# All four gate groups of the last chunk ahead of its value groups

## The chip, the cores and the metric

The kernel runs on one core of one Trainium2 chip. The metric is device time in microseconds (us) of one execution; less is better. Beside it stands a profile of one execution, whose span runs from the first to the last recorded instruction. Engines are called PE (TensorE, matmuls), PEld (its weight loads), DVE (VectorE), ACT (ScalarE), POOL (GpSimd) and SP (SyncE, which here issues transfers). L551 is line 551 of the kernel.

## The reference

An attention over 32 memory slots, followed by a channel mix with a gate. The change lies in the channel mix:

```python
def _moe_ref(x, mu_k, mu_r, w_k, w_v, w_r):
    x_prev = np.concatenate([np.zeros((B, 1, D)), x[:, :-1, :]], axis=1)
    xk = mu_k * x + (1.0 - mu_k) * x_prev
    xr = mu_r * x + (1.0 - mu_r) * x_prev
    k = np.maximum(xk @ w_k, 0.0)
    v = k * k @ w_v
    r = 1.0 / (1.0 + np.exp(-(xr @ w_r)))
    return (r * v).astype(np.float32)
```

Here x is the attention's output with 8 batches of 576 tokens and 512 channels, w_k is 512 x 1024, w_v 1024 x 512 and w_r 512 x 512. Tokens are independent once xk and xr are there.

## The kernel before

Attention runs per batch and writes xk and xr, transposed and in bf16, into two rings in on-chip memory. The channel mix works through the 4608 tokens in NCH = 9 chunks of 512. Each chunk has 16 groups of work, one per step of a schedule:

- eight **key** groups k0 to k7 (L510 to L524): 128 of the 1024 inner channels each. PE makes `pk` (L518, 4 matmuls of 512 columns), ACT takes the ReLU (L522), DVE squares it into `sq` (L523).
- four **gate** groups g0 to g3 (L526 to L541): 128 tokens each. PE makes `pr` (L532, 4 matmuls), ACT reads it with an exponential (L537). After every second gate ACT finishes the pair's sigmoids `sg` with a logarithm (L539) and an exponential (L540) over both.
- four **value** groups v0 to v3 (L543 to L555): 128 tokens each. PE makes `pv` from `sq` (L551, 8 matmuls), DVE multiplies it with the gate into `o` (L553), and `store` sends `o` to memory. In the last chunk v3 is made in two halves of 256 columns, each with its own accumulator, product and stores.

The schedule is a list of steps with positions, sorted before anything is emitted (L562 to L572). Channel mix step s stands at position s, so chunk c has positions 16c to 16c + 15. Attention steps have positions written out by hand in FIRST and STEADY, relative to their batch: those of the last batch reach position 118 at most, and the last chunk, c = 8, begins at 128. Within each engine instructions run in the order in which they are emitted. The order of gates and values within a chunk is the string on L558.

Accumulators come from tags with a fixed number of buffers, taken in turn: `pk` has two, `at` (attention) three, and gates and values share the three of tag `pv` (L529, L549). A group that takes a buffer waits until its previous user has been read: a gate's by L537, a value's by L553. `sg` has two buffers of two gates each, `sq` one for a chunk, and `o` three (L545); a value group waits until the stores of the value group three before it have landed.

`store` (L490 to L502) splits a block of 128 tokens into pieces by where they lie in the output; here each block has two. SP issues them all, except that for the last two blocks of the program (v2 and v3 of the last chunk) the second piece goes to ACT's queue:

```python
            eng.dma_start(out=dst, in_=o[p:p + n, cols])
            if t >= NTOK // 128 - 2:
                eng = nc.scalar
```

So the last chunk has ten stores: two each of v0, v1 and v2, and two for each half of v3.

Of the kernel before, what the change touches and what calls it, by code (L numbers as in the profile page):

```python
# [62 lines left out]
def kernel(  # L63
# [27 lines left out]
    NCH = NTOK // CT  # L91
# [398 lines left out]
    def store(o, t, cols):  # L490
        g = t * 128
        eng = nc.sync
        while g < (t + 1) * 128:
            b, r = divmod(g, S)
            p = g - t * 128
            j, p0 = divmod(r, QR)
            n = min(QR - p0, (t + 1) * 128 - g)
            dst = out[b].rearrange("(p j) d -> p j d", j=NQ)[p0:p0 + n, JT[j], cols]
# [3 lines that stand above are left out]
            g += n  # L502

    def channel_mix(c):
        t0 = c * CT
        wrap = RING - t0 % RING
        pieces = [(0, CT)] if wrap >= CT else [(0, wrap), (wrap, CT)]
        st = {}

        def key(fi):  # L510
            def go():
                if "sq" not in st:
                    st["sq"] = work.tile([128, NF, CT], BF16, name="sq", tag="sq", bufs=1)
                pk = psum.tile([128, CT], F32, name="pk", tag="pk", bufs=2)
                for lo, hi in pieces:
                    c0 = (t0 + lo) % RING
                    for di in range(ND):
                        nc.tensor.matmul(pk[:, lo:hi], lhsT=wk_sb[:, di, fi * 128:(fi + 1) * 128],  # L518
                                         rhs=xk_T[:, di, c0:c0 + hi - lo],
                                         start=(di == 0), stop=(di == ND - 1))  # L520
                rl = work.tile([128, CT], BF16, name="rl", tag="rl", bufs=3)
                nc.scalar.activation(rl, pk, AF.Relu)  # L522
                nc.vector.tensor_mul(st["sq"][:, fi, :], rl, rl)  # L523
            return go  # L524

        def gate(ts):  # L526

            def go():
                pr = psum.tile([128, Dm], F32, name="pr", tag="pv", bufs=3)  # L529
                c0 = (t0 + ts * 128) % RING  # L530
                for di in range(ND):
                    nc.tensor.matmul(pr, lhsT=xr_T[:, di, c0:c0 + 128],  # L532
                                     rhs=wr_sb[:, di, :], start=(di == 0), stop=(di == ND - 1))
                if ts % 2 == 0:
                    st[ts // 2] = work.tile([128, 2, Dm], F32, name="sg", tag="sg", bufs=2)
                sg = st[ts // 2]
                nc.scalar.activation(sg[:, ts % 2], pr, AF.Exp, scale=-1.0)  # L537
                if ts % 2 == 1:
                    nc.scalar.activation(sg, sg, AF.Ln, bias=1.0)  # L539
                    nc.scalar.activation(sg, sg, AF.Exp, scale=-1.0)  # L540
            return go  # L541

        def value(ts):  # L543
            def go():
                o = work.tile([128, Dm], F32, name="o", tag="o", bufs=3)  # L545
                n = 2 if c == NCH - 1 and ts == 3 else 1
                for h in range(n):
                    cols = slice(h * Dm // n, (h + 1) * Dm // n)
                    pv = psum.tile([128, Dm], F32, name="pv", tag="pv", bufs=3)  # L549
                    for fi in range(NF):  # L550
                        nc.tensor.matmul(pv[:, cols], lhsT=st["sq"][:, fi, ts * 128:(ts + 1) * 128],  # L551
                                         rhs=wv_sb[:, fi, cols], start=(fi == 0), stop=(fi == NF - 1))
                    nc.vector.tensor_mul(o[:, cols], st[ts // 2][:, ts % 2, cols], pv[:, cols])  # L553
                    store(o, t0 // 128 + ts, cols)
            return go  # L555

        groups = [key(fi) for fi in range(NF)]
        order = "g0 g1 g2 g3 v0 v1 v2 v3" if c == 0 else "g0 g1 v0 v1 g2 g3 v2 v3"  # L558
        return groups + [(gate if o[0] == "g" else value)(int(o[1])) for o in order.split()]


# [5 lines left out]
    for s in range(16 * NCH):  # L567
        if s % 16 == 0:
            groups = channel_mix(s // 16)
        todo.append((s, -1, 0, groups[s % 16]))  # L570
# [32 lines left out]
```

The softmax here doesn't subtract the row's maximum and nothing guards it: scores larger than these inputs give would overflow.

## Time and profile before

| | us |
|---|---|
| median of 4 runs | 224.73 (224.24 to 225.82) |
| the profiled execution | 224.94 |
| its span | 223.1 |
| PE busy in the span | 205.9 (92%) |
| ACT busy | 160.0 (72%) |
| DVE busy | 142.4 (64%) |
| 320 key matmuls, L518 | 69.4 |
| 144 gate matmuls, L532 | 35.2 |
| 296 value matmuls, L551 | 66.3 |

The granted clock of PE is full throughout (1.000). A matmul's recorded length (358 to 379 ns) is longer than its spacing, since matmuls overlap. In the chain of waits, which counts each stretch once, 8 gate matmuls in a row take 1.73 us and 16 value matmuls 3.45 us.

The lines shown below are of four kinds. A timeline row has its start, the time that the merged instructions took, engine, line, operation, output and input, and in brackets how long the engine had been idle and what released it. A row of stages has start and end, then for each engine busy time and number of instructions, the granted clock, the DMA engines' busy share and GB/s. A row of one line's instructions gives the least, median and greatest duration in ns and the first and last start. An engine with a q at its end (SPq, ACTq) is that engine's queue of issued transfers.

### The profile page before, as it was taken

What the parts mean: (1) busy time and instruction counts of PE and PEld (TensorE: products, weight loads), DVE (VectorE), ACT (ScalarE), POOL (GpSimd) and SP (SyncE); (2) the same over time, 40 slices, a digit from 0 to 9 for tenths busy, and PEclk for the clock granted to TensorE, in tenths of its full rate; (3) what the DMA queues carried; (4) which work ended last, traced back from release to release, by engine and by line L of the source; (5) the groups of instructions that cost most, each with busy time, mean ns of one, the idle gap of its engine ahead of it and who ended that gap; (6) DMA issues with size and microseconds to landing.
All of it is one profiled execution on the core that took longest, in us unless ns stands there. A gap on an engine that the chain in (4) does not pass through costs nothing.

```text
span 223.1 us, 4576 instructions
## 1 busy us (share of the span) xinstructions
PE 205.9 (92%) x1755; PEld 101.7 (46%) x1755; DVE 142.4 (64%) x356; ACT 160.0 (72%) x309; POOL 47.6 (21%) x66
## 2 busy tenths in 40 slices
PE   4269999899999998999999999999999999999991
PEld 1243345445444554445445764444443444444450
DVE  3162855297456989688777698769875974435222
ACT  2107568982899849997799679977978856855760
POOL 7554351644240638122500000000000000000000
PEclk9999999999999999999999999999999999999999
DMA  6999999999999999999994300330132033033033
GB/s 133 189 200 207 235 204 212 224 223 276 218 238 198 265 209 204 232 205 299 132 187 103 94 3 0 94 97 1 33 102 58 0 94 94 3 94 94 0 94 94
DMA packets 43349, 31.49 MB, mean 141 GB/s; under 512 B 10952, under 2 KB 37840, under 8 KB 43328
## 3 DMA queue, kind: packets, MB, share of 16 engines
q0 software_dynamic: 35248, 20.91, 62.7%
q1 hardware_dynamic: 7776, 9.97, 15.7%
q10 hardware_dynamic: 304, 0.33, 0.4%
q8 instruction: 13, 0.21, 0.4%
q14 instruction: 8, 0.07, 0.1%
HBM read 38.54 MB, written 9.44 MB: 215 GB/s over the span
## 4 chain that ended last, share of the span: by engine, by line
PE 80%; ACT 6%; DVE 5%; DMA 3%; POOL 1%; issue 1%; SPq 1%; DVEq 0%; POOLq 0%
PE pk L518 28%; PE pv L551 25%; PE pr L532 13%; DMA mu_b<-in_moe_mu_r_dram 3%; PE qtps L325 2%; PE kvps L264 2%; PE nops L382 2%; PE idle L209 2%; PE zps L355 2%; PE scps L341 1%; DVE atn L369 1%; PE mxps L439 1%; DVE o L553 1%; ACT e L345 1%; PE zps L274 1%
## 5 line engine op out<-in xcount | busy, mean ns | idle before, releaser
L518 PE MATMUL pk<-xkT,wk 128*128 128x512 bf16 (+1 forms) x320 | 69.4, 358 | 0.0
L551 PE MATMUL pv<-wv,sq 128*128 128x512 bf16 (+1 forms) x296 | 66.3, 373 | 0.0
L522 ACT ACTIVATE rl<-pk 128x512 bf16<-128x512 f32 x72 | 43.1, 601 | 27.0 <-PE pk L518 26.7
L523 DVE TENSOR_TENSOR sq<-rl 128x512 bf16<-128x512 bf16 x72 | 30.4, 423 | 25.9 <-ACT rl L522 25.5
L553 DVE TENSOR_TENSOR o<-sg,pv 128x512 f32<-128x512 f32 (+1 forms) x37 | 24.0, 672 | 31.6 <-ACT sg L540 25.6
L551 PEld LDWEIGHTS <-sq 128*128 128x128 bf16 x296 | 28.6, 98 | 32.0 <-issue 0.2
L518 PEld LDWEIGHTS <-wk 128*128 128x128 bf16 x320 | 29.0, 98 | 26.2 <-issue 1.6
L532 PE MATMUL pr<-wr,xrT 128*128 128x512 bf16 x144 | 35.2, 379 | 0.0
L537 ACT ACTIVATE sg<-pr 128x512 f32<-128x512 f32 x36 | 21.8, 605 | 8.6 <-PE pr L532 8.4
L532 PEld LDWEIGHTS <-xrT 128*128 128x128 bf16 x144 | 13.3, 98 | 15.9 <-issue 1.2
L539 ACT ACTIVATE sg<-sg 128x1024 f32<-128x1024 f32 x18 | 19.0, 1057 | 0.6
L540 ACT ACTIVATE sg<-sg 128x1024 f32<-128x1024 f32 x18 | 19.0, 1057 | 0.6
L345 ACT ACTIVATE e<-scps 128x288 bf16<-128x288 f32 x32 | 10.8, 428 | 8.1 <-PE scps L341 8.1
L407 DVE TENSOR_SCALAR mu_d<-diff,mu 128x576 bf16<-128x576 bf16 x48 | 16.4, 383 | 0.2
L386 ACT CAST x<-nops 128x288 bf16<-128x288 f32 x48 | 16.0, 416 | 0.0
L328 DVE COPY qT<-qtps 128x576 bf16<-128x576 bf16 x32 | 13.4, 450 | 1.3 <-PE qtps L325 1.3
L369 DVE TENSOR_TENSOR atn<-e,lz 128x576 bf16<-128x576 bf16 (+1 forms) x20 | 12.3, 634 | 2.9 <-ACT lz L362 2.5
L325 PE MATMUL qtps<-identity,q 96*128 96x96 bf16 x192 | 12.4, 215 | 1.2 <-DMA q<-in_q_dram 1.2
L325 PEld LDWEIGHTS <-q 96*128 96x128 bf16 x192 | 10.9, 103 | 4.7 <-DMA q<-in_q_dram 1.4
L357 ACT ACTIVATE lz<-zps 128x288 f32<-128x288 f32 x32 | 11.2, 412 | 1.2 <-PE zps L355 1.2
L362 ACT ACTIVATE lz<-lz 128x576 f32<-128x576 f32 (+1 forms) x20 | 11.4, 596 | 0.0
L248 ACT ACTIVATE em<-phm 128x1024 bf16<-128x1024 f32 x8 | 8.4, 1055 | 3.2 <-DMA phm<-in_phi_dram 3.2
(66 smaller groups left out, 187.2 us busy)
## 6 DMA issues: line engine op xcount, KB each, us to landing
out_dram<-o SPq DMA_DIRECT2D x23, 192.0 KB, 2.3
kv<-in_k_dram POOLq DMA_DIRECT2D x8, 512.0 KB, 12.4
q<-in_q_dram POOLq DMA_DIRECT2D x7, 576.0 KB, 15.0
phm<-in_phi_dram POOLq DMA_DIRECT2D x7, 512.0 KB, 12.9
kv<-in_v_dram POOLq DMA_DIRECT2D x7, 512.0 KB, 13.2
out_dram<-o SPq DMA_DIRECT2D x23, 128.0 KB, 2.4
out_dram<-o SPq DMA_DIRECT2D x23, 64.0 KB, 2.0
wk<-in_moe_w_k_dram POOLq DMA_DIRECT2D x2, 512.0 KB, 12.6
```

The source lines that it names most:

```text
L325: nc.tensor.matmul(ps[:, i, j], rhs=identity[:QR, :QR], is_transpose=True, lhsT=qs[b % 2][:, 2 * pr + i, 2 * j:2 * j + 2, :].rearrange("p ...
L386: nc.scalar.copy(st["x"][:, 2 * c + jj, sl], pss[jj])
L407: nc.vector.tensor_scalar_mul(t[:, i], st["d"][:, pr + i, :], mu1[:, o:o + 1])
L518: nc.tensor.matmul(pk[:, lo:hi], lhsT=wk_sb[:, di, fi * 128:(fi + 1) * 128], rhs=xk_T[:, di, c0:c0 + hi - lo], start=(di == 0), stop=(di = ...
L522: nc.scalar.activation(rl, pk, AF.Relu)
L523: nc.vector.tensor_mul(st["sq"][:, fi, :], rl, rl)
L532: nc.tensor.matmul(pr, lhsT=xr_T[:, di, c0:c0 + 128], rhs=wr_sb[:, di, :], start=(di == 0), stop=(di == ND - 1))
L537: nc.scalar.activation(sg[:, ts % 2], pr, AF.Exp, scale=-1.0)
L539: nc.scalar.activation(sg, sg, AF.Ln, bias=1.0)
L540: nc.scalar.activation(sg, sg, AF.Exp, scale=-1.0)
L551: nc.tensor.matmul(pv[:, cols], lhsT=st["sq"][:, fi, ts * 128:(ts + 1) * 128], rhs=wv_sb[:, fi, cols], start=(fi == 0), stop=(fi == NF - 1))
L553: nc.vector.tensor_mul(o[:, cols], st[ts // 2][:, ts % 2, cols], pv[:, cols])
```

## The change

In the last chunk, the order of the eight groups behind the keys becomes that of the first chunk: all four gates, then all four values. No other chunk and no instruction of a group is edited.

```diff
         groups = [key(fi) for fi in range(NF)]
-        order = "g0 g1 g2 g3 v0 v1 v2 v3" if c == 0 else "g0 g1 v0 v1 g2 g3 v2 v3"
+        order = "g0 g1 g2 g3 v0 v1 v2 v3" if c in (0, NCH - 1) else "g0 g1 v0 v1 g2 g3 v2 v3"
         return groups + [(gate if o[0] == "g" else value)(int(o[1])) for o in order.split()]
```

## The prediction

> **What bounds the kernel now.** I read the page first: busy shares, then the chain that ended last, to see which engine a moved group could free.
>
> ```profile
> PE 205.9 (92%) x1755; PEld 101.7 (46%) x1755; DVE 142.4 (64%) x356; ACT 160.0 (72%) x309; POOL 47.6 (21%) x66
> PE 80%; ACT 6%; DVE 5%; DMA 3%; POOL 1%; issue 1%; SPq 1%; DVEq 0%; POOLq 0%
> ```
>
> PE is the bound of the whole, and the change gives it the same matmuls. So only two things can move: gaps on PE inside the last chunk, and what follows PE's last matmul. The next view is busy time by stage: keys of the last chunk (200.90 on), its first half, its second half, the stores, the close of the program.
>
> ```profile
> 200.90:207.80 6.90, 6.90 (x33) 3.14 (x32) 3.46 (x9) 4.18 (x7) 0.00 (x0) 1.00 0.29 76
> 207.80:213.00 5.20, 5.20 (x25) 2.35 (x24) 1.29 (x3) 3.90 (x5) 0.00 (x0) 1.00 0.00 0
> 213.00:218.20 5.20, 5.17 (x32) 2.94 (x30) 1.36 (x4) 3.31 (x4) 0.00 (x0) 1.00 0.33 101
> 218.20:221.80 3.60, 0.00 (x0) 0.00 (x0) 0.70 (x3) 0.00 (x0) 0.00 (x0) 1.00 0.50 146
> 221.80:223.10 1.30, 0.00 (x0) 0.00 (x0) 0.00 (x0) 0.00 (x0) 0.00 (x0) 1.00 0.00 0
> ```
>
> After the span's start and the length come PE, PEld, DVE, ACT and POOL, then the granted clock, the DMA share and GB/s. PE has no gap from 200.9 to 218.2, so the change can take none away. But 4.9 us lie behind PE's last matmul. The timeline of the last chunk shows what they wait for.
>
> ```profile
> 209.56 0.60 ACT L537 ACTIVATE sg<-pr 128x512 f32<-128x512 f32 x1 [0.27 <-PE pr L532]
> 210.19 1.06 ACT L539 ACTIVATE sg<-sg 128x1024 f32<-128x1024 f32 x1
> 211.28 1.06 ACT L540 ACTIVATE sg<-sg 128x1024 f32<-128x1024 f32 x1
> 212.36 1.34 DVE L553 TENSOR_TENSOR o<-sg,pv 128x512 f32<-128x512 f32 x2 [3.48 <-ACT sg L540]
> 212.81 1.89 PE L532 MATMUL pr<-wr,xrT 128*128 128x512 bf16 x8
> ...
> 214.74 0.60 ACT L537 ACTIVATE sg<-pr 128x512 f32<-128x512 f32 x1 [0.27 <-PE pr L532]
> 215.37 1.06 ACT L539 ACTIVATE sg<-sg 128x1024 f32<-128x1024 f32 x1
> 216.46 1.06 ACT L540 ACTIVATE sg<-sg 128x1024 f32<-128x1024 f32 x1
> 217.54 1.35 DVE L553 TENSOR_TENSOR o<-sg,pv 128x512 f32<-128x512 f32 x3 [3.84 <-ACT sg L540]
> ```
>
> The second half's gates leave PE at 214.7; ACT takes until 217.52 to make the sigmoids. The sums of v2 were complete near 216.43 and wait for ACT, not PE. So three products start together at 217.54, and three pairs of stores follow close behind. The instructions of the storing line from 219.3 on, with the least, median and greatest duration in ns:
>
> ```profile
> L499 SPq DMA_DIRECT2D out_dram<-o x2: 372/450/528, 218.8 to 219.5; - x2
> L499 ACTq DMA_DIRECT2D out_dram<-o x2: 392/566/739, 218.9 to 219.8; - x2
> DMA to landing us min/median/max: 2.0/2.2/2.4
> ```
>
> The last product ends at 218.90, yet its ACT store starts only at 219.75: it stands behind the stores of v2 (218.26, 0.56 us) and of v3's first half (218.91, 0.74 us). It lands at 219.75 + 2.0, near 221.8, and the closing 1.3 us follow.
>
> **What the Trainium skill says.** "PSUM — Partial Sum Buffer", Specifications: eight banks, 512 FP32 values each. The code's tags (3 `at`, 2 `pk`, 3 `pv`) take all eight; the fourth gate therefore reuses a bank. The same page, Engine vs sequencer instructions: the queues of ScalarE and VectorE are strict FIFO. The trace agrees: ACT runs L537, L537, L539, L540 in program order. "Perfetto Trace Analysis", DMA Instruction — HWDGE: the profiled length of an issue is descriptor generation, not data movement. The trace agrees: v2's issue ends at 218.73, while the DMA share is zero until 219. "DMA: Bandwidth & Descriptors", Issuing engines are not separate DMA queues: stores from SP and ACT share the same 16 DMA engines. Here their share was 0.92 to 0.98 from 219.5 to 221.0.
>
> **The change part by part.** No instruction is added or removed. In chunk 8, g2 and g3 (8 matmuls, 1.73 us in the chain) move ahead of v0 and v1 (16 matmuls, 3.45 us). ACT's eight gate instructions keep their order; DVE's five products and the ten stores (seven issued by SP, the last three others by ACT) keep theirs too. All attention steps of the last batch have positions below 128, where this chunk's first key group stands, so nothing else is crossed; POOL's queue is empty here.
>
> PE, from the pitch of 0.216 us a matmul: g0 and g1 end at 209.52 as before; g2 at 210.39, g3 at 211.25, v0 at 212.98. The ring of three banks goes g0 A, g1 B, g2 C, g3 A, v0 B, v1 C, v2 A, v3's halves B and C. g3 wants A at 210.22; ACT read it by 209.29. v0 wants B at 211.09, free at 210.16. v1 wants C, g2's bank, at 212.81. That is the one new wait: g2's L537 is ready to run at 210.4 but stands behind the first pair's L539 and L540, so it runs 212.37 to 212.97 (0.60). A wake-up was 0.03 (ACT end 217.52 to DVE 217.54), so v1 starts near 213.0: **PE loses 0.2 us**. The trace does not show this wait. Below I bound it by 0.15 (the read alone), above by 0.4 (a weight load of 0.1 and a slow wake-up of 0.1 on top). Queued behind it on PE are v1 to v3, whose delay I carry through. All later banks are free: A after g3's L537 at 213.60 for v2 at 214.7; B after v0's product at 213.7 for v3 at 216.5; C after v1's product at 215.6 for 217.3.
>
> ACT: 212.97 + 0.03 + 0.60 + 0.03 + 1.06 + 0.03 + 1.06 puts the second pair's sigmoids at 215.8, 1.7 us earlier than 217.52. So v2 to v3 now wait for PE.
>
> DVE and stores, with 0.2 of delay: v2's sums end at 216.63, product (0.69) to 217.35, stores from 217.38, SP busy to 217.85, ACT to 217.94. v3's first half: PE 217.50, product (0.41) to 217.95, stores from 217.98; SP is free at 218.51, ACT (0.74) at 218.72, and 0.1 lies between two issues on it. v3's second half: PE 218.37, product to 218.82, both stores at 218.85. **The last store starts 0.90 earlier** (219.75 - 218.85): 0.08 of it from the product, the rest because its queue is free by then. The first of the six, v2's, starts 0.88 earlier (218.26 - 217.38), so even if the DMA engines and not the issues set the end, the same 512 KB begin and end about 0.9 earlier.
>
> Output buffers: v3's `o` reuses v0's, which waits for v0's stores; these start at 213.7 and 214.2 and land within 2.3, by 216.5, and v3 wants it at 217.5: 1.0 us of cover; if that were gone, the excess would fall on the end one for one. v0's product itself moves from 212.36 to 213.0; nobody waits for it but that buffer and bank B.
>
> Landing: I keep 2.0 us, the value of the same store before, since the six stores follow each other as closely as before. Bounds: 1.6, the least of this line's stores (then 1.3 us gained in all), and 2.5, near the 2.7 of the worst (then 0.4 gained). Then the closing 1.3 us, unchanged.
>
> Sum: span 223.1 - 0.9 = 222.2. The profiled execution took 224.94, so 1.84 lie around the span, and the same execution would take 224.04; the median of the runs, 224.73, is 0.21 below that execution, so **223.8**. PE's stall is already inside the 0.9.
>
> **The rivals.** A: the forecast, 223.8, 60%. B: the last stores land in 1.6; gain 1.3, **223.4**, 21%. For it: SP's last store now has 0.3 us free ahead of it and ACT's 0.1, so the engines may have drained more of the earlier ones. Against it: the six still start within 1.5 us, as before. C: the saved issue time is hidden anyway: the last store lands as late after the product as it did before (221.8 - 218.90 = 2.9), because the engines and not the queue made it late; then only the product's 0.08 is left, **224.6**, 12%. For it: DMA share above 0.9 after 219.5; against it: the transfers begin 0.88 earlier as well. D, slower: v1's bank is not freed by g2's first ACT pass but by the end of ACT's second pair, at 215.8 (if the bank order or the wait reaches to g3's whole sequence). PE would then stall 215.8 - 212.8 = 3.0 instead of 0.2, and the end comes 2.8 - 0.9 = 1.9 later: **226.6**, 7%. It costs more than it brings from a stall of 1.1 on. Against it: before, v1 reused g0's bank although L539 and L540 of that pair had not finished, with no gap on PE. That the order isn't changed at all can be excluded: the diff replaces the string for exactly this chunk.
>
> **How the numbers follow.** The range is 223.2 to 224.6: gains of 0.4 to 1.3 us give 223.4 to 224.3, widened by 0.2 to 0.3 for the scatter of a median (runs from 224.24 to 225.82), and it takes in B and C. A change of 0.5%, 1.12 us, is about what a measurement of this kernel can tell from none; faster than that means below 223.61. Of A's 60 about 19 lie there (a landing of 1.8 or less, or the scatter), of B's 21 about 20: faster 39%. Slower is D less a remainder of mild cases: 6%. The rest, 55%, is within.
>
> **What would show it.** On PE one gap of about 0.2 us ahead of v1 near 212.8, released by ACT L537, and none else in the chunk. L540's last pass ending near 215.8. DVE's product of v2 near 216.7, released by PE, and the last product ending near 218.8. First stores on ACT at 217.4, the last at 218.9, landing near 220.9; a span of 222.2. The forecast is wrong if the last store still starts after 219.3, if its landing takes 2.7 or more, or if PE stalls for over 1 us.

## The result, and the profile after

The changed kernel took 224.05 us in the median of 31 runs (223.16 to 225.2); beside them the kernel before took 225.33 in 50 runs (224.2 to 226.35). The ratio is 0.9951, with a 95% interval of 0.9940 to 0.9961: about 1.1 us less. (The two medians, over unequal numbers of runs, differ by 1.28 us; the text goes by the ratio.) The span of the profiled execution fell from 223.1 to 222.0 us.

First the busy shares of the changed kernel, then its stages: keys, the first and second part of the gates and values, the landing of the last stores, the close of the program. The columns are those of the same view before.

```profile
PE 206.0 (93%) x1755; PEld 101.8 (46%) x1755; DVE 142.6 (64%) x356; ACT 159.7 (72%) x309; POOL 47.7 (21%) x66
```

```profile
200.90:207.80 6.90, 6.90 (x33) 3.13 (x32) 3.44 (x8) 4.39 (x8) 0.00 (x0) 1.00 0.29 76
207.80:213.00 5.20, 5.20 (x25) 2.33 (x24) 0.60 (x2) 4.60 (x7) 0.00 (x0) 1.00 0.00 0
213.00:218.20 5.20, 4.98 (x31) 2.84 (x29) 2.48 (x5) 2.17 (x3) 0.00 (x0) 1.00 0.35 102
...
218.50:220.70 2.20, 0.00 (x0) 0.00 (x0) 0.00 (x0) 0.00 (x0) 0.00 (x0) 1.00 0.68 208
220.70:222.00 1.30, 0.00 (x0) 0.00 (x0) 0.00 (x0) 0.00 (x0) 0.00 (x0) 1.00 0.00 0
```

PE has the same work. What moved is ACT and DVE: ACT's busy time in the stage up to 213 grew from 3.90 to 4.60 us and in the next fell from 3.31 to 2.17, while DVE's in that stage grew from 1.36 to 2.48. The products were spread over the last microseconds instead of standing at their end. The timeline of the changed kernel's last chunk shows it:

```profile
209.94 1.06 ACT L539 ACTIVATE sg<-sg 128x1024 f32<-128x1024 f32 x1
210.62 1.82 PEld L551 LDWEIGHTS <-sq 128*128 128x128 bf16 x9
210.84 7.14 PE L551 MATMUL pv<-wv,sq 128*128 128x512 bf16 x40
211.03 1.06 ACT L540 ACTIVATE sg<-sg 128x1024 f32<-128x1024 f32 x1
211.99 1.07 ACT L537 ACTIVATE sg<-pr 128x512 f32<-128x512 f32 x2
...
213.09 1.06 ACT L539 ACTIVATE sg<-sg 128x1024 f32<-128x1024 f32 x1
213.54 5.25 SPq L499 DMA_DIRECT2D out_dram<-o  x7
214.18 1.06 ACT L540 ACTIVATE sg<-sg 128x1024 f32<-128x1024 f32 x1
...
216.33 1.24 DVE L553 TENSOR_TENSOR o<-sg,pv 128x512 f32<-128x512 f32 x2 [1.10 <-PE pv L551]
217.05 1.87 ACTq L499 DMA_DIRECT2D out_dram<-o  x3
218.02 0.42 DVE L553 TENSOR_TENSOR o<-sg,pv 128x256 f32<-128x256 f32 x1 [0.45 <-PE pv L551]
```

The second pair's sigmoids end at 214.18 + 1.06 = 215.24. The product of v2 starts at 216.33 and is released by PE, where before it started at 217.54 and was released by ACT. The first store on ACT leaves at 217.05 instead of 218.26. The last, from the instructions of the storing line between 218.2 and 219.0, leaves at 218.5 instead of 219.75:

```profile
L499 ACTq DMA_DIRECT2D out_dram<-o x2: 390/557/724, 217.7 to 218.5; - x2
L499 SPq DMA_DIRECT2D out_dram<-o x1: 317/317/317, 218.5 to 218.5; - x1
DMA to landing us min/median/max: 2.0/2.2/2.4
```

One thing has to be taken out before two executions are compared. The chain of waits of the changed kernel says where the gates begin, that is, where the keys of the last chunk end:

```profile
204.96 2.59 PE pk L518 x12
207.55 3.45 PE pr L532 x16
211.00 6.99 PE pv L551 x40
```

Before, that point was 207.79:

```profile
207.79 1.73 PE pr L532 x8
```

So 0.24 of the 1.1 us between the spans had come about ahead of the change. I call the time from that point to the end of the span the tail; from the trace's records it is 15.34 us before and 14.50 after, 0.84 less. Times of single stores, here and below, are read from the same records.

### The profile page after: what moved, and what is told of

The parts are those of the page before. It is cut to its first block, busy times and chain, and to the rows that moved or that the text cites. A ratio compares the mean times of both kernels' runs of the same rounds, so it can differ in the third digit from the quotient of the medians.

```text
span 222.0 us, 4576 instructions
## 1 busy us (share of the span) xinstructions
PE 206.0 (93%) x1755; PEld 101.8 (46%) x1755; DVE 142.6 (64%) x356; ACT 159.7 (72%) x309; POOL 47.7 (21%) x66
## 4 chain that ended last, share of the span: by engine, by line
PE 82%; DVE 5%; ACT 4%; DMA 3%; POOL 1%; issue 1%; SPq 1%; DVEq 0%; POOLq 0%
PE pk L518 28%; PE pv L551 27%; PE pr L532 13%; DMA mu_b<-in_moe_mu_r_dram 3%; PE qtps L325 2%; PE kvps L264 2%; PE nops L382 2%; PE idle L209 2%; PE zps L355 2%; PE scps L341 1%; PE mxps L439 1%; DVE atn L369 1%; DVE o L553 1%; ACT e L345 1%; PE zps L274 1%
## 5 line engine op out<-in xcount | busy, mean ns | idle before, releaser
L553 DVE TENSOR_TENSOR o<-sg,pv 128x512 f32<-128x512 f32 (+1 forms) x37 | 24.2, 672 | 31.3 <-ACT sg L540 18.3
L537 ACT ACTIVATE sg<-pr 128x512 f32<-128x512 f32 x36 | 21.6, 604 | 6.8 <-PE pr L532 6.5
L540 ACT ACTIVATE sg<-sg 128x1024 f32<-128x1024 f32 x18 | 19.0, 1057 | 0.6
L539 ACT ACTIVATE sg<-sg 128x1024 f32<-128x1024 f32 x18 | 19.0, 1057 | 0.6
L369 DVE TENSOR_TENSOR atn<-e,lz 128x576 bf16<-128x576 bf16 (+1 forms) x20 | 12.3, 633 | 2.9 <-ACT lz L362 2.5
## 6 DMA issues: line engine op xcount, KB each, us to landing
kv<-in_k_dram POOLq DMA_DIRECT2D x8, 512.0 KB, 12.3
wk<-in_moe_w_k_dram POOLq DMA_DIRECT2D x2, 512.0 KB, 12.3
```

## The experiments

The theory: the second pair's sigmoids used to be late, and all six last stores with them. The rivals put the gain on PE's order, on a wait that any chunk has, on the DMA engines rather than the queues, or ahead of the last chunk. Each ratio is to the kernel before, run on the same chip. "Keys end" is the first gate matmul in the chain of waits. A tail comes from one trace each. How far it repeats can be seen twice: "again" is within 0.07 us of the changed kernel, and chunk7, whose last chunk is that of the kernel before, is within 0.06 of the kernel before.

| run | ratio, 95% interval | keys end, us | tail, us |
|---|---|---|---|
| kernel before | 1 | 207.79 | 15.34 |
| changed kernel | 0.9951 (0.9940 to 0.9961) | 207.55 | 14.50 |
| again | 0.9961 (0.9948 to 0.9974) | 207.71 | 14.43 |
| pass1 | 0.9966 (0.9949 to 0.9983) | 207.79 | 14.48 |
| pass2 | 1.0003 (0.9985 to 1.0020) | 208.59 | 15.59 |
| chunk7 | 1.0008 (0.9988 to 1.0028) | 207.41 | 15.40 |
| mid | 0.9968 (0.9951 to 0.9985) | 207.90 | 14.51 |
| sp_only | 1.0001 (0.9981 to 1.0021) | 208.48 | 15.37 |
| halves | 0.9957 (0.9937 to 0.9976) | 207.88 | 14.20 |
| halves_b | 0.9999 (0.9978 to 1.0021) | 207.28 | 15.50 |
| exps | 0.9959 (0.9943 to 0.9974) | 208.13 | 14.30 |
| both | 0.9941 (0.9915 to 0.9968) | 208.38 | 14.17 |

**A dose of the lateness: pass1 and pass2.** Into the changed kernel, with n = 1 or 2:

```diff
                 nc.scalar.activation(sg[:, ts % 2], pr, AF.Exp, scale=-1.0)
+                if c == NCH - 1 and ts == 3:
+                    for _ in range(n):
+                        spare = work.tile([128, 2, Dm], F32, name="spare", tag="spare", bufs=1)
+                        nc.scalar.activation(spare, sg, AF.Exp)
```

> The changed kernel with one more ACT pass (about 1.0 us, into a spare tile) between g3's exponential and the second pair's L539. Theory (the gain is that the second pair's sigmoids are ready before v2's sums): they end near 216.3 instead of 215.2, still level with v2's sums at 216.3, so nothing is lost: ratio to the kernel before 0.995 to 0.996. Rival (any ACT work behind the gates is on the path to the end): the whole pass is paid, ratio 0.999 to 1.000.

> The same with two more passes. Theory: the sigmoids end near 217.2, so v2's product waits 0.9 us for ACT as in the kernel before, the stores start 0.9 later and nearly the whole gain is gone: ratio 0.999 to 1.000. Rival (the gain comes from the order of the matmuls on PE and its buffers, not from ACT): it stays at 0.995 to 0.996.

Timelines of the two kernels near v2's product, where L544 is the old L540 and L557 the old L553; pass1 first:

```profile
213.33 1.06 ACT L541 ACTIVATE spare<-sg 128x1024 f32<-128x1024 f32 x1
...
215.51 1.06 ACT L544 ACTIVATE sg<-sg 128x1024 f32<-128x1024 f32 x1
216.60 1.21 DVE L557 TENSOR_TENSOR o<-sg,pv 128x512 f32<-128x512 f32 x2 [1.12 <-ACT sg L544]
```

```profile
214.13 2.15 ACT L541 ACTIVATE spare<-sg 128x1024 f32<-128x1024 f32 x2
...
217.40 1.06 ACT L544 ACTIVATE sg<-sg 128x1024 f32<-128x1024 f32 x1
218.49 1.35 DVE L557 TENSOR_TENSOR o<-sg,pv 128x512 f32<-128x512 f32 x3 [2.21 <-ACT sg L544]
```

With one pass the product is now released by ACT, but at 216.60 - 207.79 = 8.81 us after the keys, against 216.33 - 207.55 = 8.78 in the changed kernel: the slack was just used up, and the tail stays. With two it starts at 9.90 and three products stand together again, as in the kernel before at 9.75, and the whole gain is gone, although PE's order is that of the changed kernel. The first pass hid entirely, the second cost 1.1 us. The ratio of pass1, 0.9966, lies a little above the expected 0.995 to 0.996, but its interval takes these in and excludes the rival's 0.999. That is the mechanism, shown with a dose, and the rivals "any ACT work" and "PE's order" fall.

**The same edit elsewhere: chunk7.**

```diff
-        order = "g0 g1 g2 g3 v0 v1 v2 v3" if c == 0 else "g0 g1 v0 v1 g2 g3 v2 v3"
+        order = "g0 g1 g2 g3 v0 v1 v2 v3" if c in (0, NCH - 2) else "g0 g1 v0 v1 g2 g3 v2 v3"
```

> The kernel before with the same reordering in the last chunk but one instead of the last. Theory (only what follows PE's last matmul is shortened): nothing, ratio 0.999 to 1.001. Rival (four gates ahead of the values spare a wait in any chunk): ratio 0.995 to 0.997.

The tail begins behind the edited chunk, so here the ratio decides: 1.0008, with an interval that excludes the rival's 0.995 to 0.997. In this chunk, which has another behind it, late products cost nothing that can be measured. The theory's reason is that PE goes on with the next keys.

**Another order with early sigmoids: mid.** To the kernel before:

```diff
         order = "g0 g1 g2 g3 v0 v1 v2 v3" if c == 0 else "g0 g1 v0 v1 g2 g3 v2 v3"
+        if c == NCH - 1:
+            order = "g0 g1 v0 g2 g3 v1 v2 v3"
```

> The last chunk in the order g0 g1 v0 g2 g3 v1 v2 v3. Theory: the second pair's sigmoids end by 215.8, before v2's sums, so it keeps the gain but for a wait of up to 0.25 us on PE ahead of v1, whose buffer is v0's: ratio 0.995 to 0.997. Rival (all four gates must stand together on PE): ratio 0.999 to 1.000.

Ratio 0.9968, tail 14.51. What counts is that both gates of the second pair come early enough, not that four stand together.

**One queue for the stores: sp_only.** In the changed kernel (the removed lines shift the later ones by two):

```diff
-            if t >= NTOK // 128 - 2:
-                eng = nc.scalar
```

> The changed kernel with all ten stores of the last chunk on SP. Theory one (the time an issue takes in its queue sets the last store): six issues of about 0.5 us in one row from 217.0 on put the last at about 219.6 instead of 218.5, so 0.9 to 1.1 us is lost: ratio 0.999 to 1.000. Theory two (the 16 shared engines set the end): 0.3 us or less is lost: ratio 0.995 to 0.997.

The instructions of the storing line from 217.9 us on:

```profile
L499 SPq DMA_DIRECT2D out_dram<-o x6: 371/448/596, 218.0 to 220.7; - x6
...
DMA to landing us min/median/max: 1.6/1.9/2.4
```

Products and matmuls stand where the changed kernel has them (last product 218.95, which is 10.47 after the keys in both), yet the last store starts at 220.7, 12.2 after the keys instead of 11.0, and 0.87 us of tail is lost again. So the row of issues in one queue sets the end here, and not the engines' transfer: by the records the last store landed a little faster (1.9 us after its start, against 2.2) but far too little to make up for it. Nor do busy engines seem to stretch an issue. In the kernel before, ACT's issue at 218.91 took 0.74 us while the engines' share was zero up to 219.0 and 0.18 from there to 219.5; its issue of an equal store at 219.75 took 0.39 with the share above 0.9. Why equal stores differ so is not shown. The row of issues also explains why the last product's own advance, 0.21 us counted from the keys' end, is the smaller part of the gain.

**Smaller pieces: halves and halves_b.** The same edit in the changed kernel and in the kernel before:

```diff
-                n = 2 if c == NCH - 1 and ts == 3 else 1
+                n = 2 if c == NCH - 1 and ts >= 2 else 1
```

> The changed kernel with v2 made in two halves like v3, so that 128 KB leave every 0.87 us. Theory (the last landing of 2.2 us holds a wait for the data of the stores before it): the last store starts as before and lands in 1.7 to 1.9: 0.3 to 0.5 us more, ratio 0.993 to 0.994. Rival (a landing takes what it takes, whatever else is under way): ratio 0.995, or 0.996 for the two more stores.

> The kernel before with v2 made in two halves. Theory: both halves wait for the late sigmoids until 217.5, and then two more stores stand ahead of the last ones in the queues: 0.3 to 0.8 us slower, ratio 1.001 to 1.004. Rival (halving helps by itself, without earlier sigmoids): ratio 0.998 or less.

In halves the last store started 0.04 us earlier, counted from the keys' end, and landed in 2.0 instead of 2.2: the expected 1.7 to 1.9 was missed, and the larger part of the landing isn't a wait for other stores' data. The tail is 0.30 shorter in the one trace: about 0.04 by the start, 0.13 by the landing and 0.14 by the closing stretch, which the theory did not touch. The ratio cannot be told from the changed kernel's. In halves_b the expected loss of 0.3 to 0.8 us did not show: the ratio is 0.9999, and the tail grew by 0.16. Its timeline shows a wait that I had not counted, v3's second half for v2's first product, whose buffer it takes:

```profile
217.03 1.08 DVE L553 TENSOR_TENSOR o<-sg,pv 128x256 f32<-128x256 f32 x3 [3.84 <-ACT sg L540]
...
217.50 1.03 PE L551 MATMUL pv<-wv,sq 128*128 128x256 bf16 x8 [0.69 <-DVE o L553]
```

PE stood still ahead of the last half, and yet the last store started only 0.4 us later than in the kernel before (12.3 us after the keys' end instead of 12.0): its product was ready at 218.99, but it stood behind the others in ACT's queue until 219.61.

**The wait that the change added: exps.** In the last chunk of the changed kernel:

```diff
-                if ts % 2 == 1:
-                    nc.scalar.activation(sg, sg, AF.Ln, bias=1.0)
-                    nc.scalar.activation(sg, sg, AF.Exp, scale=-1.0)
+                if c == NCH - 1:
+                    pairs = [st[0], st[1]] if ts == 3 else []
+                else:
+                    pairs = [sg] if ts % 2 == 1 else []
+                for p in pairs:
+                    nc.scalar.activation(p, p, AF.Ln, bias=1.0)
+                    nc.scalar.activation(p, p, AF.Exp, scale=-1.0)
```

> The changed kernel with the exponentials of all four gates ahead of both logarithms in the last chunk, so that v1's buffer is free long before it is wanted. Theory: the gap on PE ahead of v1 (0.06 us beyond the pitch) goes and nothing else moves, since v0's product, now later by about 1 us, is waited for by nobody: ratio as for the changed kernel, 0.994 to 0.996. Rival (the later v0 holds up a buffer or a store): ratio 0.997 or more.

The chain of waits of this kernel gives the 40 value matmuls 6.94 us, against 6.99 in the changed kernel:

```profile
211.59 6.94 PE pv L555 x40
```

The wait ahead of v1 is gone and was worth 0.05. Since the edit frees v1's buffer early and changes nothing else on PE's way, it also shows what that wait was for. The rival's fear was not idle; the timeline shows v3's first product (L557, the old L553) waiting for v0's later stores:

```profile
217.78 0.42 DVE L557 TENSOR_TENSOR o<-sg,pv 128x256 f32<-128x256 f32 x1 [0.23 <-DMA out_dram<-o]
```

It comes early enough for the last product not to feel it. The ratio is that of the changed kernel. The tail is 0.20 shorter in the one trace, most of it by a landing of 2.01 us instead of 2.17.

**Repeat and combination: again and both.** The changed kernel unchanged, and halves with exps.

> The changed kernel once more, to see whether the measured 0.9951 holds more than the tail explains. From the last key matmul to the end the traces give 15.34 us before and 14.50 after, 0.84 us or 0.37%. Theory (the tail is all): ratio 0.996 to 0.997, and a tail of 14.4 to 14.6 in its trace wherever the keys end. Rival (something ahead of the last chunk is shortened too, by the 0.24 us by which the keys ended earlier): ratio 0.995 or less, and keys that end before 207.6 again.

> The changed kernel with v2 in halves and with all four gates' exponentials ahead of the logarithms. If the two gains of the single traces (tail 14.20 and 14.30 against 14.50) add up, the tail is 14.0 and the ratio 0.994 to 0.995; if both only shift the same landing of the last store, the tail is 14.2 and the ratio 0.995 to 0.996.

The repeat gives 0.9961 with a tail of 14.43 and keys that end at 207.71, so nothing ahead of the chunk is shown to be shorter. In both the tail is 14.17: the two small gains do not add up. A possible reason stands among the waits of its SP queue (0.7 us in total, once, 0.7 at the longest):

```profile
SPq L499 <- DMA out_dram<-o: 0.7, 1, 0.7
```

Its last store leaves on SP at 219.62, 11.24 us after the keys and 0.38 after its product, though the issue before it had ended at 218.84: by this view it waits for an earlier store to land, and so it starts 0.26 later than in the changed kernel. The ratio of both, 0.9941, is the lowest, but its interval holds the changed kernel's: that it is faster is not shown.

## Why the prediction was right

**The late sigmoids and the stores behind them: right.** The prediction had the second pair ready near 215.8, v2's product released by PE near 216.7, and the last store 0.90 us earlier. Counted from the keys' end the last store moved from 219.75 - 207.79 = 11.96 to 218.53 - 207.55 = 10.98, by 0.98. Pass2 makes the sigmoids late again in the same order of matmuls, and the old time comes back.

**The wait ahead of v1: in the right place, too large.** Put at 0.2 us, with 0.15 as its lower bound; measured 0.05, by exps, below that bound. The wrong term was g2's L537, set to start 0.03 after the pass before it. In the timeline after, it starts at 211.99, while L540 ends at 211.03 + 1.06 = 212.09, and two of them fit into 1.07 us instead of 1.23. I had taken the spacing of passes that wait for each other's result for that of passes that don't. With the shorter wait the last product ended 0.14 us earlier than forecast (10.89 us after the keys instead of 11.03). The last store kept only 0.08 of it: its product ends at 218.44, the issue ahead of it on ACT at 218.43, and 0.1 lies between two issues, where the forecast had the queue free a little before the product.

**The landing: a little too short.** Kept at 2.0; the last store landed near 220.7, 2.2 after its start. The earlier start and the longer landing nearly cancel: 0.98 less 0.13 more for the landing (2.04 before, 2.17 now, by the records) gives 0.85, the 0.84 of the tails. That 0.84 comes so near the forecast 0.9 is in part luck.

**The unaffected rest: right.** No other gap on PE, no wait for an output buffer, 1.3 us of closing in both.

**Rivals.** C, that issue time is hidden by the engines, falls with the trace and with sp_only: C had the last store land 2.9 us after the last product, and it landed 2.25 after it. B, a landing of 1.6, did not occur. D, a stall of 3 us, did not occur.

**The size.** The forecast was 223.8 against 224.73, a ratio of 0.996; measured were 0.9951 and 0.9961. The absolute 223.8 rests on four runs of the kernel before with a median of 224.73, where the 50 runs beside the changed kernel have 225.33, so the ratio is the better test. The forecast's likeliest outcome was a change within 0.5%; the first measurement stands at that bound. Tails give 0.9963, just outside the first interval and inside the second. Whether that remainder is more than chance stays open.

## What to carry to other kernels

At the end of a program, look for the last engine that must finish and then ask which *inputs* of the last few steps are late although another engine could have had them early: here that order mattered in the last chunk, and in the one before it, as chunk7 shows, it did not. Several stores that become ready together pay for each other's issue time in the queue. Here spreading their producers was worth more than the last product's own advance: the last store started 0.98 us earlier, its product was ready 0.21 earlier. And compare two spans from the last common point: here the keys of the last chunk, which no run edited, ended anywhere from 207.3 to 208.6 us, a spread of more than the whole effect.

## What the runs showed of the hardware that was not expected

ACT starts a pass about 0.1 us ahead of the recorded end of the previous one where it does not need its result (211.99 against 212.09 in the changed kernel), and 0.03 us behind it where it does (L540 behind L539 before: 210.19 + 1.06 = 211.25, start 211.28). That the dependence makes the difference, and not the kind of pass, shows in exps. There the first logarithm (L543, the old L539) does not need the exponential just ahead of it, while in the changed kernel it does:

```profile
211.62 0.60 ACT L537 ACTIVATE sg<-pr 128x512 f32<-128x512 f32 x1 [0.27 <-PE pr L532]
212.12 1.05 ACT L543 ACTIVATE sg<-sg 128x1024 f32<-128x1024 f32 x1
213.20 1.06 ACT L544 ACTIVATE sg<-sg 128x1024 f32<-128x1024 f32 x1
```

L543 starts 0.10 ahead of the end of L537 (212.22), and L544, which needs L543, 0.03 behind it (213.17). In pass1 a pass that only overwrites what the one before it reads keeps the 0.03 too (L541 ends at 214.39, L543 starts at 214.42). A step of such a chain therefore cost about 0.13 us more than a step between independent passes.

From its start, the last store took between 1.8 and 2.2 us to land in all traces, with the stores close together or spread out, from one queue or two.
